# Four one-bank PSUM tiles in place of two two-bank tiles, with readers of one bank each

## The chip, the cores and the metric

One core of one Trainium2 chip runs the kernel. The metric is the device time of an execution in microseconds, the median of three runs.

## The reference

```python
def _moe_ref(x, w_in, w_out):                 # 4608 x 512 tokens, 512 -> 2048 -> 512
    h = x @ w_in
    g = np.maximum(0.01 * h, h)
    return (g @ w_out).astype(np.float32)

def _moe2_ref(x, w_in, w_out, a, b):
    h = x @ w_in
    h2 = h * h
    h3 = h2 * h
    P = a[0] + a[1] * h + a[2] * h2 + a[3] * h3
    Q = 1.0 + np.abs(b[0]) * np.abs(h) + np.abs(b[1]) * h2
    g = P / (Q + 1e-06)
    return (g @ w_out).astype(np.float32)

def reference(**kwargs):
    attn_out = _attn_ref(q, k, v)             # softmax attention in chunks of 64 rows, 8 x 8 heads
    x = attn_out.transpose(0, 2, 1, 3).reshape(B * S, H * D)
    x = _moe_ref(x=x, **moe_kwargs)
    return _moe2_ref(x=x, **moe2_kwargs)
```

## The kernel before, in words

The 4608 tokens are nine blocks of 512. Every float32 operand of a matmul is split into a high part (fp32r) and a remainder, and each product is three passes: high x high, high x low, low x high (`PASSES`). The first gemm of a layer makes 128 features of 512 tokens at a time, 12 matmuls of 128x512 into one PSUM bank (`gemm1`, L551); the activation reads that bank, its result is split into gh (ScalarE) and gl (VectorE), and the second gemm adds 12 matmuls into the four banks oa, ob (`gemm2`, L583; `task`, L826).

PSUM's eight banks: four hold the sums of the second gemm (oa, ob). Two are the tile `hha` (L242), [128, 2, 512], opened at the start and kept. The last two are the attention's tile `at` until the first layer is nearly done; then it is closed, and the tile `hhb` (L1177), [128, 2, 512] too, takes its place. `hh_ps` is the list of the banks that `gemm1` goes through in turn: two banks until then, four from there on. The tile framework sets all waits from the accesses to the tiles; the order of the instructions on each engine is the order of the code (`manual_schedule`).

The program in order of time. *Start-up* (`start_up`): attention of the first blocks, the decoding of the weights and the first steps of layer one, in an order that a list planner (`ordered`) makes. *First layer* (L1130): `gemm1` of a step, attention work, the activation (L568, L574, L579), and `gemm2` of the step two before. *Second* (`second`, L734): first the 16 first gemms of the last block of layer one, one after the other, nearly without second gemms between (L890; the activation is L897). Then layer two of block 0 (L928): 16 times a `gemm1` (L931), its rational activation on 128x512 (`act_abs`, `act_lin`, `act_q`, `act_p1`, `act_p2`, then `finish_one`), and a `task`. Then the loop over u (L1015), 32 passes: 4 pairs of blocks, 8 passes each. In a pass a Strassen-like scheme makes four banks of 512 columns (two feature groups of two blocks) with seven products of six matmuls (`product`, L973; `skip_group_check` lets a product add to what a bank holds). With a = hha[:, 0], b = hha[:, 1], c = hhb[:, 0], d = hhb[:, 1], a pass is:

- a task; B11 into a; ScalarE copies a into sw0 (L1039); B21 into b; VectorE adds sw0 to b (L1044);
- T2 added into a; ScalarE copies a into sw1 (L1051); a task; T3 added into a; ScalarE copies a into s3 (L1058);
- T1 into c; VectorE writes c + s3 into d (L1063); T4 added into a; a task;
- `begin(u, 0, hha)`: |h| of both banks in one activation of 128x1024 (L860), a linear step of it (L861), and a linear step of h from both banks (L864);
- p1 of hha (L870, 128x1024); B22 added into c; VectorE adds sw1 to c (L1087); p2 of hha (L873); a task (not in passes 1, 3, 5, 7);
- `begin(u, 1, hhb)`: the same of c and d. What is left of it (p1, p2, `act_q` on GpSimd, `act_l` (L876, L877), `act_r` (L880), `act_g` (L883, L884)) is done in the next pass, mixed with the same of hha.

`pre` (L822) puts the split into gh (L814) and gl (L815) for the tasks to come between these; `x_split` (L770) and the sums of the forms (L749) of the next pair of blocks stand in some of the passes.

Of the kernel before, what the change touches and what calls it, by code (L numbers as in the profile page):

```python
# [9 lines left out]
F32 = mybir.dt.float32  # L10
# [3 lines left out]
AF = mybir.ActivationFunctionType  # L14
# [3 lines left out]
P = 128  # L18
# [196 lines left out]
def tile_kernel(ctx: ExitStack, tc: tile.TileContext, qt, kt, vt, w1, w2, a, b, out):  # L215
# [16 lines left out]
    def ps_open(nm, side="left"):  # L232
        ps_pools[nm] = tc.tile_pool(name=nm, bufs=1, side=side, space=bass.MemoryType.PSUM, reuse_waits="tile")
        return ps_pools[nm].__enter__()

    def ps_close(nm):
        ps_pools.pop(nm).__exit__(None, None, None)

    def singles(pool, *names):
        return [pool.tile([P, 512], F32, name=nm) for nm in names]  # L240

    hha = ps_open("hhp").tile([P, 2, 512], F32, name="hha")  # L242
    hh_ps = [hha[:, j] for j in range(2)]
    at2 = ps_open("atp", "right").tile([P, 2, 512], F32, name="at")
    at_ps = [at2[:, j] for j in range(2)]
    startp = ps_open("startp")
# [15 lines left out]
    absb = const.tile([P, 2], F32, name="absb")  # L262
# [471 lines left out]
    def second(npool):  # L734
        S, G = nc.scalar, nc.gpsimd

        def ntile(k, name, shape=(P, 2, TM)):
            return npool.tile(list(shape), F32, tag=f"n{k}", name=name)

        def blocks_of(j):  # L740
            return 1 + 2 * j, 2 + 2 * j
# [28 lines left out]
        def x_split(j, n):  # L770
            t = xform[j, FORMS[n]]
            S.activation(out=t[:, 0], in_=t[:, 1].bitcast(F32), func=AF.Copy)
            V.tensor_tensor(out=t[:, 1], in0=t[:, 1].bitcast(F32), in1=t[:, 0].bitcast(F32), op=ALU.subtract)
# [48 lines left out]
        def pre(ahead=1):  # L822
            while halved[0] < min(done[0] + ahead, len(tasks)):
                split()
# [34 lines left out]
        def act_abs(h, ah, u):  # L859
            S.activation(out=ah, in_=h, func=AF.Abs)  # L860
            S.activation(out=u, in_=ah, func=AF.Identity, scale=absb[:, 1:2], bias=absb[:, 0:1])  # L861

        def act_lin(h, t):
            S.activation(out=t, in_=h, func=AF.Identity, scale=nega[:, 3:4], bias=nega[:, 2:3])  # L864

        def act_q(ah, u):
            G.tensor_tensor(out=u, in0=u, in1=ah, op=ALU.mult)  # L867

        def act_p1(h, t):
            V.tensor_tensor(out=t, in0=t, in1=h, op=ALU.mult)  # L870

        def act_p2(h, t):
            V.scalar_tensor_tensor(out=t, in0=t, scalar=nega[:, 1:2], in1=h, op0=ALU.add, op1=ALU.mult)  # L873

        def act_l(u, l):
            S.activation(out=l, in_=u, func=AF.Abs_reciprocal_sqrt, bias=cst[:, 0:1])  # L876
            S.activation(out=l, in_=l, func=AF.Square)  # L877

        def act_r(u, l):
            V.scalar_tensor_tensor(out=u, in0=u, scalar=C1, in1=l, op0=ALU.add, op1=ALU.mult)  # L880

        def act_g(u, l, t):
            V.scalar_tensor_tensor(out=u, in0=u, scalar=2.0, in1=l, op0=ALU.subtract, op1=ALU.mult)  # L883
            V.scalar_tensor_tensor(out=t, in0=t, scalar=nega[:, 0:1], in1=u, op0=ALU.add, op1=ALU.mult)  # L884
# [5 lines left out]
        for f in range(NF):  # L890
# [5 lines left out]
            t = g8[f // 2][:, f % 2]  # L896
# [25 lines left out]
        def finish_one(s):  # L922
            u, t = chain.pop(s)
            act_l(u, tmp[:, 1])
            act_r(u, tmp[:, 1])
            act_g(u, tmp[:, 1], t)

        for s in range(NF):  # L928
# [3 lines left out]
            k, x = divmod(s, 2)  # L932
# [14 lines left out]
            t, u = pair[:, x], us[:, x]  # L947
# [32 lines left out]
                        skip_group_check=not start,  # L980
                    )

        def begin(u, c, h):
            sub = free.pop(0)
            t = make[sub]()
            left_of[sub] = 2
            i = blocks_of(u // HALF)[c]
            for x in range(2):
                ready[1, i, 2 * (u % HALF) + (x if c else 1 - x)] = t[:, x], sub
            ah, uu = ntile(4, f"ah{u}_{c}"), ntile(5 + c, f"u{u}_{c}")  # L990
            live[u, c] = h, ah, uu, t
            act_abs(h, ah, uu)
            act_lin(h, t)

        def on(u, c, what):
            if (u, c) not in live:
                return
            h, ah, uu, t = live[u, c][:4]
            if what == "q":
                act_q(ah, uu)  # L1000
            elif what == "p1":
                act_p1(h, t)
            elif what == "p2":
                act_p2(h, t)
            elif what == "l":
                live[u, c] += (ntile(7 + c, f"l{u}_{c}"),)
                act_l(uu, live[u, c][4])
            elif what == "r":
                act_r(uu, live[u, c][4])
            else:  # L1010
                act_g(uu, live.pop((u, c))[4], t)

        a, b, c, d = hha[:, 0], hha[:, 1], hhb[:, 0], hhb[:, 1]
        skip = (1, 3, 5, 7)
        for u in range(NU2):  # L1015
            j, k = divmod(u, HALF)
            v, head, tail = u - 1, j > 0 and k == 0, j + 1 < NPAIRS and k == HALF - 1
            X = {nm: xform[j, nm] for nm in FORMS if (j, nm) in xform}
            pre()
            task()  # L1020
            if u == 0:
                finish_one(NF - 1)
            on(v, 1, "q")
            on(v, 0, "l")
            on(v, 1, "p1")
            on(v, 1, "p2")
            pre()
            if head:
                x_split(j, 4)
            if j + 1 < NPAIRS and 2 <= k < 6:  # L1030
                sums_make(j + 1, k - 2, st[j + 1, k - 2], G)
            if j + 1 < NPAIRS and 1 <= k < 5:
                st[j + 1, k - 1] = ntile(3, f"st{j + 1}_{k}", (P, 4, 256))
                sums_load(j + 1, k - 1, st[j + 1, k - 1])
            sw, s3 = ntile(9, f"s{u}"), t0pool.tile([P, TM], F32, tag="t0", name=f"s3_{u}")
            product(wb[u][:, :, 0:256], X["B11"], a, True, True)
            if tail:
                x_load(j + 1, 2)
            S.activation(out=sw[:, 0], in_=a, func=AF.Copy)  # L1039
            product(wb[u][:, :, 256:512], X["B21"], b, True, True)  # L1040
            if tail:
                x_load(j + 1, 3)
            on(v, 0, "r")
            V.tensor_tensor(out=b, in0=b, in1=sw[:, 0], op=ALU.add)  # L1044
            if head:
                x_split(j, 5)
            product(wa[u][:, 1], X["T2"], a, False, True)
            if tail:
                x_load(j + 1, 4)
            on(v, 1, "l")  # L1050
            S.activation(out=sw[:, 1], in_=a, func=AF.Copy)  # L1051
            on(v, 0, "g")
            task()
            pre()
            product(wa[u][:, 2], X["T3"], a, False, True)
            if tail:
                x_load(j + 1, 5)
            S.activation(out=s3, in_=a, func=AF.Copy)  # L1058
            product(wa[u][:, 0], X["T1"], c, True, True)
            if tail:  # L1060
                x_load(j + 1, 6)
            on(v, 1, "r")
            V.tensor_tensor(out=d, in0=c, in1=s3, op=ALU.add)  # L1063
            on(v, 1, "g")
            if head:
                x_split(j, 6)
            product(wb[u][:, :, 512:768], X["T4"], a, False, True)
            if u + 2 < NU2:
                load_b(u + 2)
            task()  # L1070
            pre()
            if j + 1 < NPAIRS and k in (4, 5):
                x_load(j + 1, k - 4)
            if j + 1 < NPAIRS and k in (5, 6):
                x_split(j + 1, k - 5)
            if tail:
                x_split(j + 1, 2)
                x_split(j + 1, 3)
            begin(u, 0, hha)
            on(u, 0, "q")  # L1080
            if u not in skip:
                pre(2)
            on(u, 0, "p1")
            product(wa[u][:, 3], X["B22"], c, False, True)
            if u + 2 < NU2:
                load_a(u + 2)
            V.tensor_tensor(out=c, in0=c, in1=sw[:, 1], op=ALU.add)  # L1087
            on(u, 0, "p2")
            if u not in skip:
                task()  # L1090
            begin(u, 1, hhb)

        u = NU2 - 1
        pre()
# [19 lines left out]
    with tc.manual_schedule(), tc.tile_pool(name="tpool", bufs=1) as t0pool:  # L1114
        with tc.tile_pool(name="apool", bufs=2) as apool, tc.tile_pool(name="rpool", bufs=2) as rpool:
# [14 lines left out]
            for s, (i, f, first, last) in enumerate(STEPS[:-NF]):  # L1130
# [4 lines left out]
                u = ubase[i + 1] + k  # L1135
# [26 lines left out]
                j, e = STEPS[s - L1][:2]  # L1162
# [11 lines left out]
                    stage_w()  # L1174

        ps_close("atp")
        hhb = ps_open("hhq", "right").tile([P, 2, 512], F32, name="hhb")  # L1177
        hh_ps.extend(hhb[:, j] for j in range(2))
        with tc.tile_pool(name="npool", bufs=1) as npool:
            second(npool)  # L1180
    for nm in ("hhq", "accp", "hhp"):
# [48 lines left out]
```

## Time and profile before

| | |
|---|---|
| runs of the kernel before | 1861.8 us median of 3 (1861.3 to 1865.17) |
| the profiled execution | 1862.72 us, span from first to last instruction 1860.9 us |
| TensorE busy | 1689.2 us (91%), 9198 matmuls |
| VectorE busy | 1210.2 us (65%), 1697 instructions |
| ScalarE busy | 909.7 us (49%), 1290 instructions |
| GpSimd busy | 257.7 us (14%) |
| chain that ended last | PE 66%, ACT 18%, DVE 11%, issue 4%, DMA 1% |
| granted TensorE clock, mean | 0.958 |

In the profile PE is TensorE (PEld its weight loads), DVE is VectorE, ACT ScalarE, POOL GpSimd, SP the engine that issues the DMAs. L976 is line 976 of the kernel. A matmul's row shows where it starts and a modelled end; where matmuls follow each other without a gap, the distance of the starts is what each one costs. "idle" is the time in which the engine stood still just before an instruction, and behind the arrow stands the instruction whose end ended that. The granted clock is TensorE's, 1.00 for full speed. Names of tiles are without numbers: u, l, s, sa, sb, gn are buffers in SBUF; sa, sb and gn hold the activation's numerator and result.

### The profile page before, as it was taken

To read this page: it belongs to the slowest core of one execution; us is meant where nothing else is said; L and a number is where in the kernel's file an instruction comes from. 1 tells how busy PE (TensorE), PEld (TensorE's weight loads), DVE (VectorE), ACT (ScalarE), POOL (GpSimd) and SP (SyncE) were. 2 spreads that over 40 slices of the span, in tenths; PEclk is the share of its full clock that TensorE was granted. 3 is DMA by queue.
4 is the path that set the end of the run, shared out by engine and by line. 5 is a ranking of instruction groups with operands and counts; after the bars stand their busy time and mean duration, and the time that the engine had idled before them with its cause. 6 is when DMAs were issued, how large, how long until landed. Compare 5 with 4: busy or idle time off the path is not lost.

```text
span 1860.9 us, 23956 instructions
## 1 busy us (share of the span) xinstructions
PE 1689.2 (91%) x9198; PEld 1350.4 (73%) x9198; DVE 1210.2 (65%) x1697; ACT 909.7 (49%) x1290; POOL 257.7 (14%) x157
## 2 busy tenths in 40 slices
PE   8999999999999999989888887888888888788879
PEld 7888888888888888867666675676666666566667
DVE  7894666566665666327656666767677677766762
ACT  7653333333333333237655645655565565665552
POOL 0000000000000000001213311323112331122110
PEclk9999999999999999999998888999889899899989
DMA  7531234333434333255445644666456566445325
GB/s 261 204 103 56 81 116 127 129 118 123 132 114 130 114 125 114 88 179 170 153 147 187 212 149 153 214 203 207 160 175 207 171 221 205 137 161 168 132 90 181
DMA packets 143569, 284.69 MB, mean 153 GB/s; under 512 B 12384, under 2 KB 45408, under 8 KB 138208
## 3 DMA queue, kind: packets, MB, share of 16 engines
q1 hardware_dynamic: 143024, 282.51, 45.7%
q8 instruction: 73, 1.20, 0.3%
q10 hardware_dynamic: 432, 0.66, 0.1%
q14 instruction: 40, 0.33, 0.1%
HBM read 229.64 MB, written 53.48 MB: 152 GB/s over the span
## 4 chain that ended last, share of the span: by engine, by line
PE 66%; ACT 18%; DVE 11%; issue 4%; DMA 1%; POOL 0%; DVEq 0%; ACTq 0%; SPq 0%; POOLq 0%
PE hha L559 21%; PE hha L976 11%; PE oa L592 10%; PE ob L592 9%; PE oa L837 5%; PE ob L837 4%; ACT u L861 3%; ACT ah L860 3%; DVE gl L815 3%; PE hhb L976 2%; ACT l L876 2%; ACT gh L814 2%; PE hhb L559 2%; ACT sa L864 1%; ACT sb L864 1%
## 5 line engine op out<-in xcount | busy, mean ns | idle before, releaser
L559 PE MATMUL hha<-x,w 128*128 128x512 f32 x1728 | 417.0, 390 | 7.7 <-DVE sa L873 2.4
L559 PEld LDWEIGHTS hha<-x,w 128*128 128x128 f32 x1728 | 323.1, 188 | 78.5 <-ACT g L897 3.3
L867 POOL TENSOR_TENSOR u<-u,ah 128x1024 f32<-128x1024 f32 x64 | 163.4, 2553 | 653.8 <-ACT u L861 653.8
L568 ACT ACTIVATE t<-hha 128x512 f32<-128x512 f32 x128 | 76.5, 597 | 317.3 <-PE hha L559 301.4
L837 PE MATMUL oa<-gh,wo 128*128 128x512 f32 x576 | 215.9, 415 | 12.0 <-DVE y L625 6.4
L976 PE MATMUL hha<-xf_B,wb 128*128 128x512 f32 x384 | 123.2, 464 | 98.0 <-ACT s L1039 94.6
L837 PE MATMUL ob<-gh,wo 128*128 128x512 f32 x576 | 202.0, 391 | 0.0
L579 DVE TENSOR_TENSOR gl<-t,gh 128x512 fp32r<-128x512 f32 x128 | 88.4, 690 | 146.7 <-ACT gh L574 142.7
L592 PE MATMUL oa<-gh,w 128*128 128x512 f32 x512 | 182.0, 396 | 0.0
L592 PE MATMUL ob<-gh,w 128*128 128x512 f32 x512 | 178.4, 389 | 0.0
L976 PEld LDWEIGHTS hha<-xf_B,wb 128*128 128x128 f32 x384 | 79.9, 218 | 130.4 <-ACT s L1039 108.1
L976 PE MATMUL hha<-xf_T,wa 128*128 128x512 f32 x384 | 122.1, 461 | 27.9 <-DVE hha L1044 27.9
L837 PEld LDWEIGHTS oa<-gh,wo 128*128 128x128 f32 x576 | 117.0, 203 | 41.8 <-DVE y L625 8.9
L976 PEld LDWEIGHTS hha<-xf_T,wa 128*128 128x128 f32 x384 | 82.0, 222 | 64.5 <-DVE hha L1044 47.9
L837 PEld LDWEIGHTS ob<-gh,wo 128*128 128x128 f32 x576 | 109.9, 191 | 23.7
L837 PE MATMUL oa<-gl,wo 128*128 128x512 f32 x288 | 120.1, 417 | 6.3 <-DVE gl L815 6.3
L487 POOL TENSOR_TENSOR e<-e,sm 128x512 f32<-128x512 f32 x23 | 24.0, 1044 | 713.7 <-DVE sm L483 713.7
L837 PE MATMUL ob<-gl,wo 128*128 128x512 f32 x288 | 112.7, 391 | 0.0
L592 PEld LDWEIGHTS oa<-gh,w 128*128 128x128 f32 x512 | 96.1, 188 | 21.1
L592 PEld LDWEIGHTS ob<-gh,w 128*128 128x128 f32 x512 | 96.1, 188 | 20.1
L592 PE MATMUL oa<-gl,w 128*128 128x512 f32 x256 | 99.9, 390 | 0.0
L495 DVE STREAM_TRANSPOSE pt<-e 32x256 f32<-32x256 f32 x224 | 97.5, 435 | 3.2
(194 smaller groups left out, 2934.3 us busy)
## 6 DMA issues: line engine op xcount, KB each, us to landing
wo<-wd SPq DMA_DIRECT2D x144, 512.0 KB, 5.2
wa<-ws SPq DMA_DIRECT2D x32, 1024.0 KB, 5.0
raw<-in_w SPq DMA_DIRECT2D x46, 512.0 KB, 4.8
wb<-wd SPq DMA_DIRECT2D x32, 512.0 KB, 4.3
q<-in_q SPq DMA_DIRECT2D x36, 256.0 KB, 3.6
raw<-in_w SPq DMA_DIRECT2D x9, 1024.0 KB, 5.8
v<-in_v SPq DMA_DIRECT2D x36, 256.0 KB, 3.8
k<-in_k SPq DMA_DIRECT2D x34, 256.0 KB, 3.8
```

The source lines that it names most:

```text
L495: nc.vector.transpose(pt[c + b:c + b + 32, :, a:a + 32], e[c + a:c + a + 32, :, b:b + 32])
L559: nc.tensor.matmul(ps, w[wp][:, 0, kc * P:(kc + 1) * P], x[:, xp, kc, :], start=(kc == 0 and (wp, xp) == (0, 0)), stop=(kc == KC - 1 and ( ...
L568: nc.scalar.activation(out=t, in_=ps, func=AF.Prelu, alpha=0.01)
L579: nc.vector.tensor_tensor(out=gl, in0=t, in1=gh.bitcast(F32), op=ALU.subtract)
L592: nc.tensor.matmul(o_acc(dc, n), w[wp][:, 1, dc * P:(dc + 1) * P], g[gp], start=(first and (wp, gp) == (0, 0)), stop=(last and (wp, gp) == ...
L814: S.activation(out=gh, in_=g, func=AF.Copy)
L815: V.tensor_tensor(out=gl, in0=g, in1=gh.bitcast(F32), op=ALU.subtract)
L837: nc.tensor.matmul(o_acc(dc, TM), w[:, wp, c] if ph else wt[0, f][wp][:, 1, c], g[gp], start=(f == 0 and (wp, gp) == (0, 0)), stop=(f == N ...
L860: S.activation(out=ah, in_=h, func=AF.Abs)
L861: S.activation(out=u, in_=ah, func=AF.Identity, scale=absb[:, 1:2], bias=absb[:, 0:1])
L867: G.tensor_tensor(out=u, in0=u, in1=ah, op=ALU.mult)
L976: nc.tensor.matmul(bank, wform[:, wp, kc * P:kc * P + P], x[:, xp, kc, :], start=start and kc == 0 and (wp, xp) == PASSES[0], stop=stop an ...
```

## The change

The pool `hhp` now gives two tiles of one bank each, `hh0` and `hh1`, and `hhq` gives `hh2` and `hh3`; a, b, c, d are these four. They lie where the halves of hha and hhb lay. What read a whole tile of 128x1024 (|h|, the linear step, p1, p2 in the loop over u) is now two instructions of 128x512, one for each bank; the linear step of |h|, `act_q`, `act_l`, `act_r` and `act_g`, which read SBUF, stay 1024 wide. Everything else keeps its code.

```diff
@@ -239,8 +239,7 @@
     def singles(pool, *names):
         return [pool.tile([P, 512], F32, name=nm) for nm in names]
 
-    hha = ps_open("hhp").tile([P, 2, 512], F32, name="hha")
-    hh_ps = [hha[:, j] for j in range(2)]
+    hh_ps = singles(ps_open("hhp"), "hh0", "hh1")
     at2 = ps_open("atp", "right").tile([P, 2, 512], F32, name="at")
     at_ps = [at2[:, j] for j in range(2)]
     startp = ps_open("startp")
@@ -980,7 +979,7 @@
                         skip_group_check=not start,
                     )
 
-        def begin(u, c, h):
+        def begin(u, c, *h):
             sub = free.pop(0)
             t = make[sub]()
             left_of[sub] = 2
@@ -989,8 +988,11 @@
                 ready[1, i, 2 * (u % HALF) + (x if c else 1 - x)] = t[:, x], sub
             ah, uu = ntile(4, f"ah{u}_{c}"), ntile(5 + c, f"u{u}_{c}")
             live[u, c] = h, ah, uu, t
-            act_abs(h, ah, uu)
-            act_lin(h, t)
+            for x in range(2):
+                S.activation(out=ah[:, x], in_=h[x], func=AF.Abs)
+            S.activation(out=uu, in_=ah, func=AF.Identity, scale=absb[:, 1:2], bias=absb[:, 0:1])
+            for x in range(2):
+                act_lin(h[x], t[:, x])
 
         def on(u, c, what):
             if (u, c) not in live:
@@ -999,9 +1001,11 @@
             if what == "q":
                 act_q(ah, uu)
             elif what == "p1":
-                act_p1(h, t)
+                for x in range(2):
+                    act_p1(h[x], t[:, x])
             elif what == "p2":
-                act_p2(h, t)
+                for x in range(2):
+                    act_p2(h[x], t[:, x])
             elif what == "l":
                 live[u, c] += (ntile(7 + c, f"l{u}_{c}"),)
                 act_l(uu, live[u, c][4])
@@ -1010,7 +1014,7 @@
             else:
                 act_g(uu, live.pop((u, c))[4], t)
 
-        a, b, c, d = hha[:, 0], hha[:, 1], hhb[:, 0], hhb[:, 1]
+        a, b, c, d = hh_ps
         skip = (1, 3, 5, 7)
         for u in range(NU2):
             j, k = divmod(u, HALF)
@@ -1076,7 +1080,7 @@
             if tail:
                 x_split(j + 1, 2)
                 x_split(j + 1, 3)
-            begin(u, 0, hha)
+            begin(u, 0, a, b)
             on(u, 0, "q")
             if u not in skip:
                 pre(2)
@@ -1088,7 +1092,7 @@
             on(u, 0, "p2")
             if u not in skip:
                 task()
-            begin(u, 1, hhb)
+            begin(u, 1, c, d)
 
         u = NU2 - 1
         pre()
@@ -1174,8 +1178,7 @@
                     stage_w()
 
         ps_close("atp")
-        hhb = ps_open("hhq", "right").tile([P, 2, 512], F32, name="hhb")
-        hh_ps.extend(hhb[:, j] for j in range(2))
+        hh_ps.extend(singles(ps_open("hhq", "right"), "hh2", "hh3"))
         with tc.tile_pool(name="npool", bufs=1) as npool:
             second(npool)
     for nm in ("hhq", "accp", "hhp"):
```

How the instructions stand. First TensorE in pass u = 10 of the loop, B11, B21 and T2 (wb10 and wa10 are the weights, xf1_B11 and so on the forms of the input; "waits" names the engines or DMA queues whose progress is waited for). Before:

```order
L976 MATMUL hha_75<-xf1_B11_8943,wb10_9540 128x512 [waits DMAHW1_49,DVE_49]
L976 MATMUL hha_75<-xf1_B11_8943,wb10_9540 128x512 x5
L976 MATMUL hha_75<-xf1_B21_9107,wb10_9540 128x512 [waits Activation_49]
L976 MATMUL hha_75<-xf1_B21_9107,wb10_9540 128x512 x5
L976 MATMUL hha_75<-xf1_T2_9323,wa10_9577 128x512 [waits DMAHW3_49,DVE_49]
L976 MATMUL hha_75<-xf1_T2_9323,wa10_9577 128x512 x5
```

After:

```order
L975 MATMUL hh0_75<-xf1_B11_8977,wb10_9606 128x512 [waits DMAHW1_49,DVE_49]
L975 MATMUL hh0_75<-xf1_B11_8977,wb10_9606 128x512 x5
L975 MATMUL hh1_76<-xf1_B21_9149,wb10_9606 128x512 [waits DVE_49]
L975 MATMUL hh1_76<-xf1_B21_9149,wb10_9606 128x512 x5
L975 MATMUL hh0_75<-xf1_T2_9381,wa10_9646 128x512 [waits DMAHW3_49,Activation_49]
L975 MATMUL hh0_75<-xf1_T2_9381,wa10_9646 128x512 x5
```

B21, the third and fourth row, waited for ScalarE and now waits for VectorE; T2, the last two, waited for a DMA and VectorE and now for the DMA and ScalarE. The order of the matmuls is the same.

Then ScalarE in the same pass, from `begin(10, 0)` on (ah is |h|, u and sb or sa the linear steps, gh the split for the tasks, l the first step of the reciprocal). Before:

```order
L860 ACTIVATE ah10_0_9896<-hha_75 128x1024 [waits PE_49]
L861 ACTIVATE u10_0_9897<-ah10_0_9896,absb_101 128x1024 [waits DVE_49,Activation_49]
L864 ACTIVATE sb_8206<-hha_75,nega_100 128x1024
L814 ACTIVATE gh_1_2_8_9902<-gn0_8981 128x512
L860 ACTIVATE ah10_1_9932<-hhb_7176 128x1024 [waits DVE_49,Pool_49]
L861 ACTIVATE u10_1_9933<-ah10_1_9932,absb_101 128x1024 [waits Activation_49]
L864 ACTIVATE sa_7512<-hhb_7176,nega_100 128x1024
L876 ACTIVATE l10_0_9950<-u10_0_9897,cst_102 128x1024
```

After:

```order
L992 ACTIVATE ah10_0_9978<-hh0_75 128x512 [waits PE_49]
L992 ACTIVATE ah10_0_9978<-hh1_76 128x512 [waits DVE_49]
L993 ACTIVATE u10_0_9979<-ah10_0_9978,absb_102 128x1024 [waits DVE_49,Activation_49]
L863 ACTIVATE sb_8208<-hh0_75,nega_101 128x512
L863 ACTIVATE sb_8208<-hh1_76,nega_101 128x512
L813 ACTIVATE gh_1_2_8_9986<-gn0_9019 128x512
L992 ACTIVATE ah10_1_10018<-hh2_7177 128x512 [waits DVE_49,Pool_49]
L992 ACTIVATE ah10_1_10018<-hh3_7178 128x512
L993 ACTIVATE u10_1_10019<-ah10_1_10018,absb_102 128x1024 [waits Activation_49]
L863 ACTIVATE sa_7514<-hh2_7177,nega_101 128x512
L863 ACTIVATE sa_7514<-hh3_7178,nega_101 128x512
L875 ACTIVATE l10_0_10038<-u10_0_9979,cst_103 128x1024
```

Each L860 and L864 is now two instructions, one per bank (L992, L863), the second abs after the first; nothing passes anything else.

Last, TensorE among the 16 first gemms of the last block in layer one (x0_8 is that block, w0_3 the weights of feature group 3). Before:

```order
L559 MATMUL hhb_7176<-x0_8_6393,w0_3_754 128x512 [waits Activation_49]
L559 MATMUL hhb_7176<-x0_8_6393,w0_3_754 128x512 x11
L559 MATMUL hha_75<-x0_8_6393,w0_4_873 128x512 x12
L559 MATMUL hha_75<-x0_8_6393,w0_5_867 128x512 [waits Activation_49]
L559 MATMUL hha_75<-x0_8_6393,w0_5_867 128x512 x11
L559 MATMUL hhb_7176<-x0_8_6393,w0_6_919 128x512 x12
```

After:

```order
L558 MATMUL hh3_7178<-x0_8_6394,w0_3_755 128x512 x12
L558 MATMUL hh0_75<-x0_8_6394,w0_4_874 128x512 [waits Activation_49]
L558 MATMUL hh0_75<-x0_8_6394,w0_4_874 128x512 x11
L558 MATMUL hh1_76<-x0_8_6394,w0_5_868 128x512 [waits Activation_49]
L558 MATMUL hh1_76<-x0_8_6394,w0_5_868 128x512 x11
L558 MATMUL hh2_7177<-x0_8_6394,w0_6_920 128x512 [waits Activation_49]
```

Before, the second gemm into each tile (groups 3 and 5) waits for ScalarE and the first into it (4 and 6) for nothing; after, group 3 waits for nothing and groups 4 and 5 for ScalarE, each into a bank that was used four gemms before.

## Rows read from the trace of the kernel before

**Rows 1.** Waits of TensorE, whole span: us in total, times, longest us.

```profile
PE hha L976 <- ACT s L1039: 94.6, 32, 4.7
PE hha L976 <- DVE hha L1044: 27.9, 32, 1.0
```

**Rows 2.** Busy time by stage: stage, its us, then each engine's, clock, DMA.

```profile
829.00:934.60 105.60, 93.01 (x400) 74.13 (x399) 71.95 (x102) 71.34 (x110) 20.66 (x16) 1.00 0.44 152
...
934.60:1800.00 865.40, 724.93 (x2833) 563.00 (x2832) 595.93 (x572) 493.46 (x574) 212.34 (x112) 0.91 0.53 175
```

**Rows 3.** Timeline of TensorE, pass u = 10: start us, us, engine, line, operation [idle before].

```profile
1201.22 1.52 PE L976 MATMUL hha<-xf_B,wb 128*128 128x512 f32 x6
1205.66 1.65 PE L976 MATMUL hha<-xf_B,wb 128*128 128x512 f32 x6 [2.91 <-ACT s L1039]
1208.23 1.65 PE L976 MATMUL hha<-xf_T,wa 128*128 128x512 f32 x6 [0.92 <-DVE hha L1044]
...
1215.16 1.52 PE L976 MATMUL hha<-xf_T,wb 128*128 128x512 f32 x6
1216.52 0.39 PE L837 MATMUL oa<-gh,wo 128*128 128x512 f32 x1
```

**Rows 4.** Timeline of ScalarE and VectorE, pass u = 10 into 11.

```profile
1216.72 1.03 ACT L860 ACTIVATE ah<-hha 128x1024 f32<-128x1024 f32 x1 [1.60 <-PE hha L976]
...
1221.98 1.21 DVE L870 TENSOR_TENSOR sb<-sb,hha 128x1024 f32<-128x1024 f32 x1
...
1223.11 0.68 DVE L1087 TENSOR_TENSOR hhb<-hhb,s 128x512 f32<-128x512 f32 x1
...
1223.71 1.26 DVE L873 SCALAR_TENSOR_TENSOR sb<-sb,nega,hha 128x1024 f32<-128x1024 f32 x1
...
1223.88 1.03 ACT L860 ACTIVATE ah<-hhb 128x1024 f32<-128x1024 f32 x1 [3.25 <-DVE hhb L1087]
...
1226.10 1.19 ACT L864 ACTIVATE sa<-hhb,nega 128x1024 f32<-128x1024 f32 x1
...
1227.19 1.13 ACT L876 ACTIVATE l<-u,cst 128x1024 f32<-128x1024 f32 x1
...
1229.32 0.61 ACT L814 ACTIVATE gh<-gn 128x512 fp32r<-128x512 f32 x1
1229.84 0.57 ACT L1039 ACTIVATE s<-hha 128x512 f32<-128x512 f32 x1
```

**Rows 5.** Timeline of TensorE, B21 and T2 of the first, a slow-clocked and the last pass.

```profile
937.51 1.65 PE L976 MATMUL hha<-xf_B,wb 128*128 128x512 f32 x6 [1.36 <-ACT s L1039]
940.03 1.66 PE L976 MATMUL hha<-xf_T,wa 128*128 128x512 f32 x6 [0.86 <-DVE hha L1044]
...
1311.38 2.92 PE L976 MATMUL hha<-xf_B,wb 128*128 128x512 f32 x6 [3.76 <-ACT s L1039]
1315.17 2.93 PE L976 MATMUL hha<-xf_T,wa 128*128 128x512 f32 x6 [0.86 <-DVE hha L1044]
...
1773.49 2.05 PE L976 MATMUL hha<-xf_B,wb 128*128 128x512 f32 x6 [2.91 <-ACT s L1039]
1776.40 2.93 PE L976 MATMUL hha<-xf_T,wa 128*128 128x512 f32 x6 [0.86 <-DVE hha L1044]
```

**Rows 6.** Groups by form: busy us, mean ns of one | idle before, releaser.

```profile
L976 PE MATMUL hha<-xf_T,wa 128*128 128x512 f32 x384 | 122.1, 461 | 27.9 <-DVE hha L1044 27.9
...
L860 ACT ACTIVATE tmp<-hha 128x512 f32<-128x512 f32 x8 | 4.8, 598 | 15.2 <-PE hha L559 11.3 <-issue 3.8
...
L864 ACT ACTIVATE sa<-hha,nega 128x512 f32<-128x512 f32 x4 | 3.0, 761 | 0.0
```

**Rows 7.** Groups by form, the first gemms of both layers on TensorE.

```profile
L559 PE MATMUL hha<-x,w 128*128 128x512 f32 x1728 | 417.0, 390 | 7.7 <-DVE sa L873 2.4 <-ACT g L897 2.1 <-DVE g L873 1.4
...
L559 PE MATMUL hhb<-x,w 128*128 128x512 f32 x192 | 47.2, 394 | 8.3 <-DVE sa L873 2.8 <-ACT g L897 2.7 <-DVE g L873 1.4
```

## The prediction

> **What bounds the kernel now.** I read the waits of TensorE first. Two lines hold nearly all of them: TensorE stood 94.6 us before matmuls of L976 until the ScalarE copy of L1039 ended, and 27.9 us until the VectorE add of L1044 ended, 32 times each, once per pass of the loop over u [rows 1]. I call the banks a, b (the halves of hha) and c, d (of hhb). [...]
>
> Then one pass in order of time, u = 10 [rows 3]. B11 goes to bank a at 1201.22 and is through its 1.5 us at 1202.74. B21 goes to bank b, which nobody has read since the pass before; all the same it starts at 1205.66, when the copy of bank *a* (L1039) has ended. T2 goes to a and starts at 1208.23, when the add on bank *b* (L1044) has ended. Each waits for a reader of the other bank of its tile. Only one of these pairs needs the order: T2 adds into a, which the copy reads. So the waits are false for the other two, and the order excerpts ahead show the change taking exactly these away: B21 waits for ScalarE no more, and T2 waits for ScalarE (the copy) instead of VectorE.
>
> Why the copy is so late is in rows 4. From the end of T4 a chain runs through ScalarE and VectorE: abs of (a, b) at 1216.72, the three activations and the gh behind it, p1 at 1221.98, the add L1087 at 1223.11, abs of (c, d) at 1223.88, its linear part at 1226.10, the two activations l from 1227.19, gh at 1229.32 and the copy at 1229.84, over at 1230.41. ScalarE keeps its order, so the copy stands behind all that. TensorE has little else to do meanwhile. The pass is a ring: T4's end, this chain of some 13.9 us, copy, [B21, add, T2], to T4 again. The change takes B21 and the add out of the ring, since they can be done before the copy ends.
>
> **The change part by part.**
>
> *B21 and L1044 leave the ring: -101.1 us.* After the change T2 starts where B21 starts now, 0.05 us behind the copy (B21 then lies in the wait). What is saved in a pass is the time from B21's start to T2's. [...] Over the 32 passes, first and last of them in rows 5, it is 3.76 to 3.80 in 13, 2.51 to 2.63 in 11 and 2.81 to 3.12 in 8, together 101.1 us.
>
> *Readers of 512 lengthen the ring: +22.1 us.* The abs, the linear part, p1 and p2 of a pair are each two instructions now: 4 more per pass on ScalarE and 4 on VectorE, 128 on each. On the ring lie the abs and linear parts of both halves of a pass, and one p1. Abs: one of 128x1024 takes 1.03 us [rows 4], one of 128x512 0.598 [rows 6]; two independent activations of 512 follow each other at 0.52 (1229.32 to 1229.84 [rows 4]), and the later one takes 0.57 (the copy, 128x512 from PSUM), so a pair takes 0.52 + 0.57 = 1.09, +0.06. Linear: 1.09 from its start to the next [rows 4]; one of 512 takes 0.761 [rows 6], less the same overlap of 0.09 is 0.67, twice 1.34, so +0.25. p1: 1.13 to the next now, VectorE's steps of 512 follow at 0.60 (1223.11 to 1223.71 [rows 4]), so +0.07. Sum 2 x (0.06 + 0.25) + 0.07 = 0.69 us, times 32 = 22.1. Without any overlap it would be 2 x (0.17 + 0.33) + 0.15 = 1.15, that is 37 us. The other added VectorE steps (p2, and the second p1) lie in VectorE's idle time: it is busy 595.9 of 865.4 us [rows 2]. If that cover goes, they join the ring at some 0.07 to 0.2 us each.
>
> What the rows show for a split is thus 0.06 us for the abs and 0.25 for the linear part. [...]
>
> *The single gemms lose their false waits: -13 us.* In the 16 gemms of the last block's first layer (up to 829 us) and the 16 of L931 behind them, every second gemm waits for the reader of the other bank of its tile: the two L559 groups stand idle 7.7 + 8.3 = 16.0 us, after the readers L897 and L873 [rows 7]. With four tiles a gemm waits for the reader four gemms back, long done. The second of these stages keeps VectorE 72.0 and ScalarE 71.3 us busy in 105.6 [rows 2], so they follow at a shorter step too, but gh, gl and the split of the forms come close; I take 13 of the 16, bounds 8 and 16.
>
> *The clock: -15 us.* A clock of 0.91 over 865.4 us is 2 x 0.09 x 865.4 = 156 us at the lower level, at most 78 us lost; 19 of them are in the 101.1 already (13 x 1.23 + 8 x 0.4), so up to 59 are left: T2 and T3 alone show 461 ns a matmul against 390 [rows 6, 7]. The lower level follows the waits: after waits for L1039 of 1.1 to 1.4 us (7 passes, the first in rows 5) B21 and T2 behind them are at full clock each time, after 2.91 us in 3 of 14, after 3.76 to 4.73 us in 0 of 11. The new wait stands before T2 and is the old one + 0.69 - 1.36 (B21's six matmuls, T4 took as many from 1215.16 to 1216.52 [rows 3]): 2.91 becomes 2.2, 3.78 becomes 3.1, 4.73 becomes 4.1, 1.1 to 1.4 become 0.4 to 0.7. For 2.2 I take half the passes, for the longer ones no change, so a quarter of the 59 comes back. Bounds: all 59 back, or 20 more lost.
>
> *Nothing:* start-up and first layer. There a gemm also waits for the reader of the other bank, but between two gemms 12 matmuls of the second gemm stand (twice a product's 1.36 us [rows 3], against a reader of 512 with its 0.6 [rows 6]), and TensorE shows no wait for L568 worth a row. Fills that no longer wait only hand the wait to the matmul behind them. SP and GpSimd keep their instructions and order; their loads start earlier with the passes.
>
> Sum against the profiled execution's own 1862.7 us (span 1860.9; the median of the runs is 1861.8, 0.9 lower): -101.1 + 22.1 - 13 - 15 = -107.0, so **1756 us**.
>
> **The rivals.**
> *The clock comes back entirely.* With one wait of 2.2 us in place of 2.91 and 0.9 the lower level may not come at all. For: 7 of 7 after short waits. Against: 11 passes keep waits of 3 to 4 us. 1756 - 44 = 1712 us.
> *VectorE and ScalarE become the ring in full.* The passes shrink from 27.0 (865.4 / 32) to some 24 us while VectorE's 18.6 grow to some 19; where two splits of the forms and the halved steps meet, gl or p1 comes late. Then the ring grows by 1.38 a pass, not 0.69 (+22), the single gemms give nothing (+13) and the clock nothing (+15): 1806 us. For: VectorE is in the ring already. Against: it idles 270 us of the loop.
> *Slower: the new wait drops the clock in every pass just before the ring's matmuls.* T2, a task, T3, T1, T4 are 36 matmuls; at the lower level each costs 0.23 us more (six span 2.93 us there against 1.52 [rows 5, 3]). Break-even is where that loss, now at most 59, rises by 92.0 (101.1 - 22.1 + 13): 151 us, or 21 of the 36 in every pass. With 27 it is 32 x 27 x 0.23 = 199 us and 1862.7 - 92.0 + 199 - 59 = 1911 us. For: 11 of 14 passes fell after 2.91 us, and now the wait is in one piece. Against: it is shorter. [...]
> *The change doesn't do what it says:* the waits would stay, 1862 us and the split steps on top. The order speaks against it.
>
> **How the numbers follow.** Forecast (1735 to 1780) 0.60; clock back entirely 0.15; VectorE and ScalarE in full 0.18; slower 0.03; no gain 0.01; the rest, between these, 0.03. The range must reach to the first two rivals: 1712 to 1806, which leaves out under 2 in 10. A change within 0.2% (3.7 us) is about what a measurement of this kernel can't tell from none: faster 0.95, same 0.02, slower 0.03.
>
> **What would show it.** Right: no idle before B21, one wait of some 2 us before T2 for the copy; passes some 2.2 to 3 us shorter; no waits at L558; 128 more instructions on ScalarE and on VectorE; a clock in the loop above 0.91. Wrong: a wait before T2 as long as the old two together with B21, VectorE waits (gl, p2) before tasks or B11 that weren't there, or a clock below 0.91.

## The result, and the profile after

The change takes **1746.84 us** (median of four runs, 1739.91 to 1753.26) beside 1862.34 for the kernel before on the same chip: a ratio of **0.938, 95% interval 0.933 to 0.943**. The forecast was 1756 us, 1712 to 1806. The profiled execution took 1752.58 us (span 1750.7), 110.1 less than that of before; its terms are worked out against that one. The runs of the change fall into two groups, some 1740 us at a mean granted clock of 0.983 and some 1753 at 0.975, and the profiled one is of the second.

The page of the change (engines; then a group of section 5: busy us, mean ns | idle before it):

```profile
PE 1653.1 (94%) x9198; PEld 1340.8 (77%) x9198; DVE 1210.7 (69%) x1825; ACT 926.6 (53%) x1418; POOL 260.4 (15%) x157
...
L558 PE MATMUL hh<-x,w 128*128 128x512 f32 x1920 | 459.9, 390 | 0.1
```

The 128 instructions more on ScalarE and on VectorE are there, and the single gemms, which stood idle 7.7 + 8.3 us [rows 7], now stand 0.1. TensorE's waits in the change (us in total, times, longest):

```profile
PE hh L975 <- ACT s L1043: 62.4, 27, 4.2
PE oa L836 <- DVE y L624: 7.6, 6, 1.7
PE oa L836 <- DVE gl L814: 6.4, 8, 1.3
```

One wait is left where two stood with 94.6 and 27.9 us [rows 1]; none stands before B21. Three stretches with the same work in both kernels, first in the kernel before, then in the change: the 16 gemms of layer one, the 16 of layer two, the loop from its first to its last product (columns as in [rows 2]; clock and DMA are the last three):

```profile
784.67:829.61 44.94, 40.13 (x169) 31.01 (x168) 9.40 (x20) 12.54 (x22) 0.00 (x0) 1.00 0.66 219
829.61:934.64 105.03, 92.44 (x398) 73.64 (x396) 71.99 (x102) 71.39 (x110) 20.66 (x16) 1.00 0.45 153
...
934.64:1789.76 855.12, 717.92 (x2803) 557.56 (x2802) 589.46 (x566) 486.50 (x567) 207.71 (x111) 0.91 0.53 176
```

```profile
781.37:819.45 38.08, 38.08 (x169) 31.53 (x168) 9.48 (x20) 12.66 (x22) 0.00 (x0) 1.00 0.78 258
819.45:917.62 98.17, 94.54 (x397) 74.39 (x396) 73.23 (x103) 71.06 (x110) 20.74 (x16) 0.98 0.49 166
...
917.62:1679.12 761.50, 683.64 (x2804) 547.33 (x2803) 588.62 (x689) 503.04 (x691) 210.22 (x111) 0.95 0.59 198
```

The start-up and first layer end 3.3 us earlier (784.67 to 781.37), the two stages of single gemms take 6.9 us less each, the loop 93.6 less; what follows it takes 0.4 more. Together that is 110.2, the difference of the spans.

A pass of the change at full clock, from T2 of u = 11 to T2 of u = 12, TensorE:

```profile
1179.46 1.66 PE L975 MATMUL hh<-xf_T,wa 128*128 128x512 f32 x6 [1.97 <-ACT s L1043]
...
1186.39 1.52 PE L975 MATMUL hh<-xf_T,wb 128*128 128x512 f32 x6
...
1197.27 2.88 PE L975 MATMUL hh<-xf_B,wb 128*128 128x512 f32 x12
1202.12 1.33 PE L975 MATMUL hh<-xf_T,wa 128*128 128x512 f32 x4 [1.97 <-ACT s L1043]
```

B11 and B21 run as one piece of twelve at 1197.27, and T2 waits 1.97 us for the copy. The pass takes 1202.12 - 1179.46 = 22.66 us.

### The profile page after: what moved, and what is told of

Read it like the earlier page. It is cut to its first block, busy times and chain, and to the rows that moved or that the text cites. A ratio compares the mean times of both kernels' runs of the same rounds, so it can differ in the third digit from the quotient of the medians.

```text
span 1750.7 us, 24111 instructions
## 1 busy us (share of the span) xinstructions
PE 1653.1 (94%) x9198; PEld 1340.8 (77%) x9198; DVE 1210.7 (69%) x1825; ACT 926.6 (53%) x1418; POOL 260.4 (15%) x157
## 3 DMA queue, kind: packets, MB, share of 16 engines
q1 hardware_dynamic: 143024, 282.51, 48.5%
## 4 chain that ended last, share of the span: by engine, by line
PE 67%; ACT 18%; DVE 10%; issue 3%; DMA 1%; POOL 0%; SPq 0%; ACTq 0%; DVEq 0%; POOLq 0%
PE hh L558 23%; PE hh L975 11%; PE oa L591 10%; PE ob L591 10%; PE oa L836 5%; PE ob L836 4%; ACT u L993 3%; DVE gl L814 3%; ACT ah L992 3%; ACT l L876 2%; ACT sa L863 2%; ACT l L875 2%; ACT gh L813 2%; ACT sb L863 1%; PE at L458 1%
## 5 line engine op out<-in xcount | busy, mean ns | idle before, releaser
L558 PE MATMUL hh<-x,w 128*128 128x512 f32 x1920 | 459.9, 390 | 0.1
L558 PEld LDWEIGHTS hh<-x,w 128*128 128x128 f32 x1920 | 359.7, 188 | 75.4 <-DVE x L543 0.5
L866 POOL TENSOR_TENSOR u<-u,ah 128x1024 f32<-128x1024 f32 x64 | 163.8, 2559 | 559.2 <-ACT u L993 556.4
L567 ACT ACTIVATE t<-hh 128x512 f32<-128x512 f32 x128 | 76.5, 597 | 315.2 <-PE hh L558 301.5
L975 PE MATMUL hh<-xf_T,wa 128*128 128x512 f32 x576 | 162.9, 432 | 62.5 <-ACT s L1043 62.4
L975 PEld LDWEIGHTS hh<-xf_T,wa 128*128 128x128 f32 x576 | 115.3, 205 | 99.1 <-ACT s L1043 75.6
L836 PEld LDWEIGHTS oa<-gh,wo 128*128 128x128 f32 x576 | 117.6, 204 | 44.9 <-DVE y L624 10.2
L992 ACT ACTIVATE ah<-hh 128x512 f32<-128x512 f32 x128 | 69.5, 596 | 126.7 <-DVE hh L1091 86.5
L591 PE MATMUL ob<-gl,w 128*128 128x512 f32 x256 | 99.6, 389 | 0.0
```

The costliest lines, as they stand in the source:

```text
L558: nc.tensor.matmul(ps, w[wp][:, 0, kc * P:(kc + 1) * P], x[:, xp, kc, :], start=(kc == 0 and (wp, xp) == (0, 0)), stop=(kc == KC - 1 and ( ...
L567: nc.scalar.activation(out=t, in_=ps, func=AF.Prelu, alpha=0.01)
L591: nc.tensor.matmul(o_acc(dc, n), w[wp][:, 1, dc * P:(dc + 1) * P], g[gp], start=(first and (wp, gp) == (0, 0)), stop=(last and (wp, gp) == ...
L836: nc.tensor.matmul(o_acc(dc, TM), w[:, wp, c] if ph else wt[0, f][wp][:, 1, c], g[gp], start=(f == 0 and (wp, gp) == (0, 0)), stop=(f == N ...
L975: nc.tensor.matmul(bank, wform[:, wp, kc * P:kc * P + P], x[:, xp, kc, :], start=start and kc == 0 and (wp, xp) == PASSES[0], stop=stop an ...
L992: S.activation(out=ah[:, x], in_=h[x], func=AF.Abs)
```

## The experiments

The kernel before ran beside each group of experiments (medians 1865 to 1868 us); the ratios are to that one. The loop is measured in each trace from its first to its last product. "Low" is the time in it in which the trace's records of the granted clock show 0.50 in place of 1.00, summed, with the number of its stretches: before 153.6 us in 22, the change 78.5 in 20. Six matmuls of a product span 2.93 us in such a stretch and 1.52 at 1.00 [rows 5, 3].

**The readers alone.** The two-bank tiles stay, what reads them is split:

```diff
-            act_abs(h, ah, uu)
-            act_lin(h, t)
+            for x in range(2):
+                S.activation(out=ah[:, x], in_=h[x], func=AF.Abs)
...
-        a, b, c, d = hha[:, 0], hha[:, 1], hhb[:, 0], hhb[:, 1]
+        a, b, c, d = hh_ps
```

> Tiles of two banks as before, only the readers of the loop over u split into 512 each. Theory (the gain is the false waits, the split itself is a cost of some 0.4 us a pass): the waits for the copy and for the add on b stay at some 95 + 28 us before matmuls and the time is 1862 + 13 = 1875 us, up to 1885 if the predicted 0.69 us a pass is right. Rival (readers one bank wide are what helps, since an add or p1 can start on one bank earlier): at most 1800 us.

1889.35 us, ratio 1.0118 (1.0099 to 1.0137): above both times that were expected. Its waits:

```profile
PE hha L976 <- ACT s L1044: 101.9, 32, 4.9
PE hha L976 <- DVE hha L1049: 27.6, 32, 0.9
```

Both false waits are there, the copy's 7.3 us longer. From the start of T4 to the end of the next pass's copy, where the split readers lie, the 31 stretches of the loop take 12.7 us more than before (486.1 and 498.8 us in total). The rest of the loop's 23.4 us lies between the copy and T4, with 191 us of the loop at the low clock in place of 153.6. So the split readers are a price, some 22 us here with what the clock adds, and the whole gain of the change comes from the tiles.

**c and d as one tile again.** The change, with c and d one two-bank tile inside the loop and readers of 1024 for it:

```diff
-        a, b, c, d = hh_ps
+        ps_close("hhq")
+        hhb = ps_open("hhr", "right").tile([P, 2, 512], F32, name="hhb")
+        a, b, c, d = *hh_ps[:2], hhb[:, 0], hhb[:, 1]
...
-            begin(u, 1, c, d)
+            begin(u, 1, hhb)
```

> The change, but in the loop over u c and d are one tile of two banks again, with readers of 128x1024. Theory (only the pair a, b had false waits that cost in the loop; c and d need theirs anyway, and their split lengthens the ring by 0.2 us a pass): no wait before B21, T2's waits shorter by 0.2, 6 us faster than the change: 1735 to 1745 us. Rival (c and d need to be apart too): T1 or B22 wait and the time is above 1755 us.

**1722.78 us**, ratio 0.9236 (0.9212 to 0.9259): more than expected. Two T2 of it:

```profile
1173.34 1.66 PE L975 MATMUL hh<-xf_T,wa 128*128 128x512 f32 x6 [1.68 <-ACT s L1047]
...
1195.72 1.65 PE L975 MATMUL hh<-xf_T,wa 128*128 128x512 f32 x6 [1.68 <-ACT s L1047]
```

The pass takes 22.38 us, 0.28 less than 22.66, some 9 us over 32. The rest is put down to the clock, which is low for 44.8 us in 11 stretches. Of the seven passes u = 10, 11, 18, 19, 26, 27, 30, seven of the thirteen in which the change waits 1.97 us, five took 24.3 us (low clock) in its profiled execution and two 22.7; here all seven took 22.4.

**The copy ahead of l.** The change, with the linear step l of the first half (L875, 128x1024, and L876) put behind the copy of a on ScalarE:

```diff
             on(v, 1, "q")
-            on(v, 0, "l")
...
             S.activation(out=sw[:, 0], in_=a, func=AF.Copy)
+            on(v, 0, "l")
```

> The change, with the two activations l of the first half (2.2 us of ScalarE) put behind the copy of a instead of ahead of it. Theory (T2 waits only since the copy stands in ScalarE's order behind l and gh): T2's wait of 1.97 us goes, passes fall from 22.7 to about 21 us, the clock in the loop rises, 1690 to 1715 us. Rival (VectorE, busy 19 us a pass, is the ring's next bound, so that r, g and gl come late): waits for gl appear before tasks and the time stays above 1735 us.

**1705.81 us**, ratio 0.9139 (0.9123 to 0.9155). Waits:

```profile
PE hh L975 <- ACT s L1042: 12.7, 15, 2.0
PE hh L975 <- DVE xf_B L772: 9.3, 3, 3.1
PE oa L836 <- DVE gl L814: 7.9, 13, 2.3
```

The copy's 62.4 us are 12.7, the loop took 714.2 us, and low clock is left in 27.3. The copy is what the pass waits for, and what stands ahead of it on ScalarE is the price.

**Work in the wait.** The change, with eight matmuls of 128x128 that add zero to an open sum, between B21 and T2; and (the bracket on u in the diff) the same without them in the seven passes in which T2 has nothing or almost nothing to wait for:

```diff
+        V.memset(ident, 0.0)
...
+            if tasks[done[0]][2] > 0 and (0 < u < 9 or u > 9 and u % 4 != 1):
+                for _ in range(8):
+                    nc.tensor.matmul(
+                        o_acc(0, TM)[:, 0:P], ident, ident, start=False, stop=False, skip_group_check=True
+                    )
             product(wa[u][:, 1], X["T2"], a, False, True)
```

> The change, with eight matmuls of zeros (128 columns, added to an open sum) between B21 and T2 in passes whose next task is not the first of a block, so that TensorE is busy in most of its wait. Theory (the low clock costs what it slows: some 1.6 us in each of about 20 passes): mean clock of the loop from 0.95 to 0.99 or more, 1715 to 1730 us. Rival (the low clock is hidden by the ring, or the fills come late): 1740 us or more.

> The change with the 8 matmuls of zeros between B21 and T2, but not in the seven passes in which T2 had no wait (u = 0, 9, 13, 17, 21, 25, 29); they add zero to an open sum. With them in every pass it took 1737.5 us, and the distance between the starts of B11 grew from 20.4 to 20.9 us to 22.2 in just these seven, some 11 us, while the passes with a wait of 1.97 us stayed at 22.67 and none of those was at the low clock. Theory: the low clock after T2's wait costs the change some 1.6 us in each pass where it comes, and the fill gave that back but paid 11 us in the seven: 1722 to 1730 us. Rival: the fill had no price there, and the clock isn't worth more than was seen: 1735 to 1740 us.

1737.49 us (0.9308, 0.9293 to 0.9322) and 1729.92 us (0.9280, 0.9264 to 0.9296). The loops, by stage, the first and the second:

```profile
918.77:1664.68 745.91, 712.08 (x3315) 589.30 (x3314) 588.80 (x688) 501.79 (x691) 210.04 (x111) 0.99 0.61 202
```

```profile
919.88:1655.05 735.17, 698.14 (x3204) 574.50 (x3203) 588.75 (x688) 501.23 (x691) 210.12 (x111) 0.99 0.62 205
```

The clock is 0.99 in place of 0.95 at the same ring: the seven passes named above all took 22.7 us. The first run fell between both expectations, since its fill cost 1.4 to 1.9 us in each of the seven passes without a wait (u = 9 took 22.24 in place of 20.88 from B11 to B11); without it there the loop is 10.7 us shorter, as the second expectation had it (the low clock can be at most 3.5 of that: it holds for 17.2 and 10.2 us), and 26.3 shorter than the change's profiled one. About that is what the low clock costs the change there.

**The change again**, for the two groups of its runs.

> The change as it is, beside the others on one chip: 1740 to 1754 us, in which a run's time goes with its clock (0.983 or 0.975). With four tiles and the copy early 1706 us, so 34 to 48 below this; the c, d tile 17 to 31 below.

1751.92 us (1740.80 to 1753.08, five runs; ratio 0.9374, 0.9346 to 0.9402). The profiled one is of the group near 1740:

```profile
917.92:1667.41 749.49, 671.52 (x2803) 538.59 (x2802) 588.98 (x689) 502.31 (x691) 210.31 (x111) 0.97 0.61 201
```

The loop is 12.0 us shorter than in the first trace of the same kernel, low for 48.5 us in place of 78.5; four in place of five of the seven passes ran low. TensorE's waits for the copy are the same in both traces (62.3 and 62.4 us), so what tells them apart is the clock.

**The same order with the tiles of before.** First the copy ahead of l alone in the kernel before; then also the VectorE add on b ahead of L880:

```diff
-            on(v, 0, "r")
             V.tensor_tensor(out=b, in0=b, in1=sw[:, 0], op=ALU.add)
+            on(v, 0, "r")
```

> The kernel before, with its two tiles of two banks and its readers of 1024, and only the linear step l of the first half put behind the copy of a. Theory: there too the copy ends the ring, so the ring is 1.1 to 1.3 us shorter in a pass (the l took 1.13), 36 to 42 us in all: 1820 to 1832 us; the false waits stay, B21 behind the copy with 50 to 60 us in place of 94.6, T2 behind the add with 28. Rival: in the ring before something else than ScalarE's order holds the copy, or the clock gives it back: 1845 us or more.

> The kernel before with its two tiles of two banks: l of the first half behind the copy of a, as in the last run of that kind (1836 us), and the step L880 (act_r) put behind the VectorE add on b, so that the add no longer stands behind it and the l. There TensorE had waited 37.7 us for the copy and then 80.8 us for the add (3.04 us in a typical pass). Theory: T2's wait was a false one for an add held by VectorE's order; with the add straight behind B21 that wait is 0.9 us again, 28 to 30 us in all, so 50 us go, and as many passes are TensorE's own then, 1780 to 1795 us; the four tiles with the copy early (1706 us) stay 75 us or more ahead, since B21 and the add still stand behind the copy. Rival: L880 moved back makes p1, p2 or gl late instead and the pass stays: 1825 us or more.

1836.09 us (0.9847, 0.9828 to 0.9866), between its expectations, and **1764.79 us** (0.9461, 0.9442 to 0.9481), better than its theory, and 59 us behind the four tiles with the copy early where 75 or more was expected. The first one's waits, and VectorE in a pass of it:

```profile
PE hha L976 <- DVE hha L1044: 80.8, 32, 3.1
PE hha L976 <- ACT s L1038: 37.7, 32, 2.6
```

```profile
1197.48 0.94 DVE L815 TENSOR_TENSOR gl<-sa,gh 128x512 fp32r<-128x512 f32 x1
1198.35 1.75 DVE L880 SCALAR_TENSOR_TENSOR u<-u,l 128x1024 f32<-128x1024 f32 x1
1200.02 0.69 DVE L1044 TENSOR_TENSOR hha<-hha,s 128x512 f32<-128x512 f32 x1
```

The second one's waits:

```profile
PE hha L976 <- ACT s L1038: 37.5, 32, 2.6
PE hha L976 <- DVE hha L1043: 36.1, 32, 1.4
```

With the copy early, its wait fell from 94.6 to 37.7 us, but the add's grew from 27.9 to 80.8: B21 now ends earlier, but on VectorE the add still stands behind gl and L880. In the pass shown L880 comes straight behind the gl; in 16 of the 31 passes that have an L880 VectorE stood still before it for the l that is now later, 0.07 to 1.79 us. T2, which needs nothing of the add, waits for it because b lies in a's tile. With four tiles the same edit had no such second wait. Once the add is put first, the add's wait is 36.1 us, and what is left is mostly 0.7 to 0.8 us before B21 (2.6 at most) and 0.9 to 1.4 before T2: short waits, after which the clock mostly holds (low 23.9 us in 3 stretches, against 75.1 in 17 in the run before it); that part the theory had left out. So order alone, with both false waits still there, gives 102 us, most of what the change gives.

**Together.** Four tiles, c and d as one in the loop, copy early; and the same with the add ahead of L880:

> c and d as one tile with readers of 1024, and the linear step l of the first half behind the copy of a: the two edits that were tried singly (1722.8 and 1705.8 us), together. Theory: with the copy put earlier the wait before T2 is 0 to 0.4 us in most passes already, so the ring no longer sets the pass and TensorE's own matmuls do; a shorter ring can then take only what is left of that wait, 12.7 us in all, and a low clock of 27 us (13.6 lost at most). 1693 to 1705 us, 0 to 13 below the copy alone. Rival: the ring still sets the pass, and the 0.28 us that a pass saves and the clock add up as they did alone (24 us): 1682 us or less.

> The fastest so far (four tiles, c and d one tile, copy early: 1701 us) with the same move of L880 behind the add on b. Theory: with four tiles nobody on TensorE waits for that add before begin, so the move changes nothing: 1699 to 1704 us. Rival: VectorE's order sets the pass there too, as gl (14.4 us of TensorE's waits) shows: 1696 us or less, or 1706 or more.

**1701.05 us** (0.9123, 0.9109 to 0.9137) and 1700.96 us (0.9122, 0.9099 to 0.9145). The waits of the first:

```profile
PE oa L836 <- DVE gl L814: 14.4, 25, 2.3
PE hhb L975 <- DVE xf_B L772: 9.3, 3, 3.1
PE hh L975 <- ACT s L1046: 7.7, 9, 1.7
```

Both went as the theories had it: the shorter ring takes 3.9 us from the loop (714.2 to 710.3) where it had been worth 9 and the clock, since hardly any of the wait was left; and with four tiles nobody waits for the add. What shows now is the task behind gl. This is the fastest version found, 51 us below the change in the same group of runs.

## Why the prediction was right

*B21 and L1044 leave the ring (-101.1), and the readers lengthen it (+22.1).* The first held. The second was too large. Every pass of the loop has three parts in both traces: T2's start to T4's, T4's start to the end of the next copy, and from there to T2. Over the loop the last part, with the first pass's B11 to T2, fell by 101.3 us. A pass at full clock went from 24.84 (T2 of u = 9 to T2 of u = 10 in the trace before) to 22.66, by 2.18 in place of 2.57 - 0.69 = 1.88 (from B21's start to T2's it is 1208.23 - 1205.66 = 2.57 us [rows 3]). The step that failed, by its size, is the **+0.69 a pass of the longer ring**. From T4's start to the copy's end it was 1230.41 - 1215.16 = 15.25 us [rows 3, 4]; in the change it is 1186.39 to 1201.49 + 0.58, that is 15.68: +0.43. Over the 31 such stretches of the loop it went from 486.1 to 497.9 us, **+11.9 in place of 22.1**, and that agrees with the 12.7 of the readers alone. The linear step's split on the first half is hidden, because behind it stood a wait that I took for a part of the chain through ScalarE. ScalarE, GpSimd and VectorE in pass u = 10 before:

```profile
1217.78 1.25 ACT L861 ACTIVATE u<-ah,absb 128x1024 f32<-128x1024 f32 x1
```

```profile
1219.10 2.40 POOL L867 TENSOR_TENSOR u<-u,ah 128x1024 f32<-128x1024 f32 x1 [10.96 <-ACT u L861]
1226.27 2.38 POOL L867 TENSOR_TENSOR u<-u,ah 128x1024 f32<-128x1024 f32 x1 [4.77 <-ACT u L861]
```

```profile
1220.67 1.38 DVE L815 TENSOR_TENSOR gl<-gn,gh 128x512 fp32r<-128x512 f32 x1 [1.50 <-ACT gh L814]
...
1227.32 1.22 DVE L870 TENSOR_TENSOR sa<-sa,hhb 128x1024 f32<-128x1024 f32 x1 [2.35 <-ACT sa L864]
```

And in the pass of the change shown above, ScalarE, GpSimd and VectorE:

```profile
1195.24 1.09 ACT L992 ACTIVATE ah<-hh 128x512 f32<-128x512 f32 x2 [3.08 <-DVE hh L1091]
1196.36 1.25 ACT L993 ACTIVATE u<-ah,absb 128x1024 f32<-128x1024 f32 x1
1197.51 1.43 ACT L863 ACTIVATE gn<-hh,nega 128x512 f32<-128x512 f32 x2
1198.83 1.15 ACT L875 ACTIVATE l<-u,cst 128x1024 f32<-128x1024 f32 x1
...
1201.49 0.58 ACT L1043 ACTIVATE s<-hh 128x512 f32<-128x512 f32 x1
```

```profile
1190.39 2.40 POOL L866 TENSOR_TENSOR u<-u,ah 128x1024 f32<-128x1024 f32 x1 [8.47 <-ACT u L993]
```

```profile
1192.20 1.15 DVE L814 TENSOR_TENSOR gl<-gn,gh 128x512 fp32r<-128x512 f32 x1 [1.80 <-ACT gh L813]
1193.27 1.27 DVE L869 TENSOR_TENSOR sa<-sa,hh 128x512 f32<-128x512 f32 x2
1194.46 0.68 DVE L1091 TENSOR_TENSOR hh<-hh,s 128x512 f32<-128x512 f32 x1
```

Before p1, VectorE does a gl. Where it starts beside no L867 it takes 0.68 to 0.77 us; here it ends 0.55 us after GpSimd's L867 (L866 in the change) in both kernels: 1222.05 - 1221.50, and 1193.35 - 1192.79. GpSimd starts when the step of |h| is through, which the linear step's split, later in ScalarE's order, doesn't touch. So of the first half only the abs counts in such a pass. The four splits that do: abs twice 0.06 (1196.36 - 1195.24 = 1.12 less 1217.78 - 1216.72 = 1.06), the second half's linear step 1198.83 - 1197.51 = 1.32 less 1.09 = 0.23, p1 1194.46 - 1193.27 = 1.19 less 1.13 = 0.06, together 0.41. Each single price was within 0.02 of the forecast's; one of them was counted that lies beside GpSimd.

*The single gemms (-13).* 13.7 us in the two stages, at 0.1 us of waits left.

*The clock (-15).* The records of the trace before have 0.50 and 1.00 alone, and 153.6 us of 0.50 in the loop where the forecast took 156. T2's start to T4's, the part that the matmuls alone set, takes 6.93 us in most passes at full clock and 8.4 us or more where the low clock falls into it. Over 32 passes it went from 259.3 us to 255.1 in the first trace of the change, 4.2 less, and to 242.6 in the second, 16.7 less. So the term isn't one number, and in the trace that the sum goes by it was too large by 10.8 us. Against 32 x 6.93 the low clock cost 37.5 us there before, not the up to 59 of the forecast. That some of it would come back and that longer waits keep the low clock was right in the main. In the two traces of the change T2 to T4 ran low after 17 of 26 waits of 1.97 us and after 13 of 16 of 2.97 to 4.15 us; it did so after none of the 14 of 1.68 us with c and d as one tile, and after none of the 0.2 us that the fill leaves. But it did so after none of the six of 2.40 to 2.53 us either (u = 2, 4, 5 in both traces).

The rival *the clock comes back entirely* gave 44 us more than the forecast; the second fill, which brings it to 0.99, came to 1730 us, 17 below the change's median.

*Slower.* The low clock halved (153.6 to 78.5 us), where this rival needed it to grow; the loop's low stretches went from 22 to 20 and, in the second trace, 15. *VectorE and ScalarE in full:* no such waits came in the change (gl 6.4 us), but they are the first line of the fastest version, where the copy's wait is nearly gone (gl 14.4 us).

*Nothing at the start* was wrong by 3.3 us; in all twelve traces the first gemm of the last block starts at 773.8 to 775.5 us with the old tiles and at 770.5 to 772.4 with the new. A false wait stands there as well, before the matmuls of zeros (L682) that fill gaps in bank 1 of hha while ScalarE's ep (L509) uses the other. Before:

```profile
PE hha L682 <- ACT ep L509: 4.0, 5, 1.6
```

After, the line is gone; 1.7 us of waits for the same ep (now L508) at L520 take its place. That these 2.3 us are most of the 3.3 is worked out, and was not tried alone. The forecast had it that a fill only hands its wait on.

**The sum.** -3.3 - 13.7 - 101.3 + 11.9 - 4.2 + 0.4 = -110.2 against the forecast's -107.0. The mechanism was right: the waits and their price are as forecast. That the time came so near is in part luck: the ring was 10.2 us too dear, the clock in this trace 10.8 too generous, and the two went against each other.

## What to carry to other kernels

The tile framework took a tile of two banks as one thing for the waits (94.6 us before B21, none there with four tiles): look in TensorE's waits for a matmul that waits for a reader of a bank it doesn't touch, and price splitting the tile by the distance between the two starts, less what the smaller readers add on the ring. Then look at what stands ahead of the awaited instruction on its in-order engine: here two moved lines were worth 102 us with the old tiles and the one for the copy 41 us beyond the new ones, and a tile that isn't falsely waited for can stay whole. A step is on the ring only if nothing else holds its successor; look for the engine that ends there last.

## What the runs showed of the hardware that was not expected

VectorE's gl, two operands in SBUF, 128x512, ended late beside GpSimd's L867 (L866 in the change) on 128x1024: in all 26 cases of either kernel's trace in which it starts beside it, it ends 0.54 to 0.56 us after GpSimd's instruction, 1.14 to 2.88 us long in place of 0.68 to 0.77, while p1 (L870), which reads PSUM, took 1.22 us at 1227.32 beside L867 and 1.21 at 1221.98 without it [rows 4]. What holds gl there no run shows.

The low clock came and went with small differences: in the two traces of the change a wait of 1.97 us before T2 was followed by it in 17 of 26 passes, and with c and d as one tile one of 1.68 us in none of 14. The wait's length alone doesn't decide: six waits of 2.40 to 2.53 us were not followed by it, nor, in the second trace, one of 3.28 us (u = 6). What does decide stays open.
